# Forming the projected rows of six weight tiles inside the attention steps of a gated two-branch attention kernel

## The chip, the cores and the metric

One core of one Trainium2 chip runs the whole program. The metric is the time of one execution on the device in microseconds (us), the median of several runs. The engines named below are TensorE (PE, with its weight loads shown apart as PEld), VectorE (DVE), ScalarE (ACT), GpSimd (POOL) and SyncE (SP), which here only issues transfers. Each engine takes its instructions in the order in which the program was written.

## The reference

Two attention layers share one input `x` (2048 rows of 576). Layer A has 32 heads of 18, each with its own key and value. Layer B has 32 query heads that share one key and one value. The two outputs are mixed row by row with a gate.

```python
def _A_ref(x, wqkv, wo):
    qkv = transpose((x @ wqkv).reshape(B, S, 3, H, Dh), 2, 0, 3, 1, 4)
    scores = einsum("bhqd,bhkd->bhqk", q, k) * Dh ** -0.5
    o = einsum("bhqk,bhkd->bhqd", softmax(scores), v)
    return transpose(o, 0, 2, 1, 3).reshape(B, S, D) @ wo
...
def _B_ref(x, wq, wk, wv, wo):
    scores = einsum("bhqd,bkd->bhqk", q, k) * Dh ** -0.5     # k, v: one head for all
    o = einsum("bhqk,bkd->bhqd", softmax(scores), v)
...
g = sigmoid((x * gate_w).sum(-1, keepdims=True))
return g * A + (1 - g) * B
```

B = 1, S = 2048, D = 576, H = 32, Dh = 18, all in float32.

## The kernel before, in words

**Numbers in two halves.** TensorE multiplies a rounded form of float32. The kernel therefore splits every operand of a projection into a rounded high part and the low rest, and adds three products (high x high, low x high, high x low). `PROJ` (line 30) lists them: 14 matmuls make one block of a projection.

**Projection.** `wall` holds 14 weight tiles of 128 columns: the shared key, the gate, the shared value, then the 32 queries of layer B, then query and key of each head of layer A. Tile `mt` of the projection gives 128 rows of a DRAM table `qk_d`, each 2048 long, high and low part. `project` (line 144) forms one block of 512 columns of such a tile: 14 matmuls, then `leave` (line 159) copies the high part on ACT, subtracts on DVE for the low part and sends both to `qk_d` from POOL's queue (512 KB in one transfer). Tiles that hold keys also store a difference of two key blocks in `kd_d`.

The program has three parts before the attention steps reach their even pace:

1. Tiles 0 to 2, four blocks each, with `x` loaded and split as they go (lines 257 to 306).
2. "Phase one": tiles 3 to 9, 28 blocks one after the other (loop at line 347, `LEAD_T = MT - 4`). After each block `bring_row` issues one load, or two after the last block of a tile, that brings finished rows from `qk_d` back into SBUF: the shared key `ksb`, its difference `kdb` and the queries `qs` of the first three heads, 27 loads in all. The weights `wv` of layer A's values are also loaded, split on ACT and DVE and stored in a DRAM table `wv_d` (`load_wv`, `store_wv`).
3. "The lead": tiles 10 to 13, 16 blocks, each followed by six row-maximum blocks of the first heads (loop at line 814). `leave_lead` does the low parts on POOL. `store_x` writes the split `x` to the DRAM table `x_d`.

**Attention steps.** There are 64 heads (u = 0 to 31 for layer B, 32 to 63 for layer A) and 16 blocks of keys each, so 1024 steps, numbered T = 16u + block. A step forms four score blocks of 128 x 512 on TensorE (`step_scores`, line 526), takes four exponentials on ACT (line 538), multiplies them with the values (`step_pv`, line 541), and forms row maxima 22 steps ahead (`step_max`, line 466: matmul, then a reduce on DVE; every second step one block goes over ACT instead, line 481). When a head's maxima are complete, at steps T with T mod 16 = 10, `max_rows` (line 489) reduces and transposes them on DVE, splits them on POOL (`mh`, lines 497 and 118), writes them to DRAM and reads them back into two rows of `qs` on SP. The first scores of that head use these rows six steps later, at T mod 16 = 0.

**Order.** The schedule is written out by hand. Three strings give the order of the operations (lines 842 to 845): `PLAIN` covers two steps; `SPARSE` covers eight steps and carries one unit `U` of other work; `DENSE` covers two steps and carries one unit. Lines 918 to 927 choose the string by the step. Units come from generators in the list `todo`, one after the other:

- `value_units` (line 417), 32 units of 14 matmuls of 288 columns: layer A's values, with weights from `wv_d` and `x` from `x_d`. Steps 10 to 265 (`VB = 10`).
- `out_proj` (line 661), first segment: 32 units of 12 matmuls of 288 columns, steps 522 to 777 (`SEG`, line 786). The second segment runs under `DENSE` from step 946 on.

`begin` (line 849) runs, every second step, what is due: the loads of the next head's rows (`load_q`, `load_k`: issued on SP at T mod 16 = 0, line 766), the loads of values, and one step of the generators in `slow`. Those are `normalise` (line 590: divides eight heads' outputs by their sums and splits them on POOL) and `prep_wo` (line 647: splits the output weights on POOL). SP issues nearly all transfers, and a transfer that has to wait holds up those behind it.

Of the kernel before, what the change touches and what calls it, by code (L numbers as in the profile page):

```python
# [8 lines left out]
F32 = mybir.dt.float32  # L9
F32R = mybir.dt.float32r  # L10
# [32 lines left out]
def gated_mix_kernel(ctx: ExitStack, tc: tile.TileContext, xT, wall, wv, wo, out):  # L43
# [3 lines left out]
    def dma(o, i, eng=None):  # L47
        o, i = (x.bitcast(F32) if x.dtype == F32R else x for x in (o, i))
        return (eng or nc.sync).dma_start(o, i)
# [19 lines left out]
    wv_d = dram.tile([2, 2, P, NKT * 288], F32, name="wv_d")  # L69
    on_d = [dram.tile([9 * P, S], F32, name=f"on{x}") for x in "hl"]  # L70


# [146 lines left out]
    def bring_row():  # L219
        if rows_back:  # L220
            rows_back.pop(0)()

    with tc.tile_pool(name="xs", bufs=1, side="right") as xsp:
# [67 lines left out]
        for c in range(4):  # L291
            for mt in range(3):
# [14 lines left out]
    vws = ExitStack()  # L307
    vwp = vws.enter_context(tc.tile_pool(name="vwp", bufs=1, side="right"))


    def load_wv(hf):
        t = vwp.tile([P, NKT, 288], F32, name="vwst")
        load5(t, wv[:, 288 * hf:288 * hf + 288])
        return t

    def store_wv(hf, st):
        w = {y: vwp.tile([P, NKT, 288], F32R, name=f"vw{y}") for y in "hl"}
        split_w(st, w, nc.vector)
        for i, y in enumerate("hl"):
            dma(wv_d[hf, i], w[y].rearrange("p k f -> p (k f)"), nc.gpsimd)  # L320

    def store_x(i):
        y, c = "hl"[i % 2], i // 2
# [7 lines left out]
    for u in range(3):  # L331
        load_q(u, put=later)

    LEAD_T = MT - 4

    def tiles_left(WN):
        for mt in range(3, MT):
            w = WN
            if mt + 1 < MT:
                WN = prep_w(W.pop(0))  # L340
            if mt + 3 < MT:
                W.append(load_w(mt + 3))
            for c in range(4):
                yield mt, c, w

    left = tiles_left(WN)
    for n in range(4 * (LEAD_T - 3)):
        mt, c, w = next(left)
        if n in (0, 10):
            vs = load_wv(n // 10)  # L350
        project(mt, c, w)
        bring_row()
        if c == 3:
            bring_row()
        if n in (8, 18):
            store_wv(n // 10, vs)
    assert not rows_back
    vws.close()


    small = ctx.enter_context(tc.tile_pool(name="small", bufs=1, side="left"))
# [35 lines left out]
    def open_ph2():  # L397
        ph1.close()
        L["pt"].append(ctx.enter_context(tc.tile_pool(name="ppool", bufs=10, side="left")))
        L["work"] = ctx.enter_context(tc.tile_pool(name="work", bufs=2, side="left"))  # L400
        p2 = ctx.enter_context(tc.tile_pool(name="p2", bufs=1, side="right"))
        L["pool"] = p2
        L["ks"] = [p2.tile([P, S], F32R, name=f"ksa{i}") for i in range(2)] + [ksb]
        L["kds"] = [p2.tile([P, 512], F32R, name="kda"), kdb]

        L["early"] = ExitStack()
        L["vx"] = L["early"].enter_context(tc.tile_pool(name="vx", bufs=1, side="right"))
        for t in L["ks"][:2]:
            for b in (SB, MB):
                dma(t[b + 54:b + 56, :], ones_r)  # L410

    def open_oacc():
        L["early"].close()
        L["oacc"] = ctx.enter_context(tc.tile_pool(name="oacc", bufs=1, side="right")) \
            .tile([P, 16, D], F32, name="oacc")

    def value_units():

        pool = L["vx"]
        XV = {}  # L420

        def load(st_):
            XV[st_] = pool.tile([P, 2 * NKT - 1, P], F32R, name="xv", bufs=2)
            dma(XV[st_], x_d[:, :, st_ * P:(st_ + 1) * P])

        load(0)
        w = [{y: pool.tile([P, NKT, 288], F32R, name=f"vw{y}{hf}") for y in "hl"} for hf in range(2)]
        for hf in range(2):
            for i, y in enumerate("hl"):
                dma(w[hf][y], wv_d[hf, i].rearrange("p (k f) -> p k f", k=NKT))  # L430
        vst = [pool.tile([P, 16, 19], F32, name=f"vst{i}") for i in range(2)]
        for t in vst:
            nc.gpsimd.memset(t, 1.0)
        yield
        for st_ in range(16):
            if st_ < 15:
                load(st_ + 1)
            x = XV.pop(st_)
            for hf in range(2):
                fp = ps_m.tile([P, 512], F32, name="pm")  # L440
                for n, (a, b, k, kr) in enumerate(PROJ):
                    nc.tensor.matmul(fp[:, 0:288], x[:kr, k if b == "h" else NKT + k, :], w[hf][a][:kr, k, :],  # L442
                                     start=(n == 0), stop=(n == len(PROJ) - 1))
                nc.scalar.activation(vst[hf][:, :, 0:18], fp[:, 0:288].rearrange("p (h d) -> p h d", d=18), AF.Copy)
                dma(v_d[st_, :, 304 * hf:304 * hf + 304], vst[hf].rearrange("p h d -> p (h d)"))
                yield
# [214 lines left out]
    def out_proj(t0, rows, first=False):  # L661

        nt = len(rows)
        oacc = L["oacc"]
# [12 lines left out]

        load(0)
        yield
        w = WO[t0]  # L680
        for q in range(8):
            if q < 7:
                load(q + 1)
            o = {y: O[q, y] for y in "hl"}
            for s2 in range(2):
                st_ = 2 * q + s2
                for hf in range(2):
                    ops = [(o[b][:r, t, s2 * P:(s2 + 1) * P], w[a][:r, t, 288 * hf:288 * hf + 288])
                           for a, b in PRODS for t, r in enumerate(rows)]
                    fp = unit_bank()  # L690
                    for n, (x, y) in enumerate(ops):
                        nc.tensor.matmul(fp[:, 0:288], x, y, start=(n == 0), stop=(n == len(ops) - 1))  # L692
                    dst = oacc[:, st_, 288 * hf:288 * hf + 288]
                    if first:
                        nc.scalar.activation(dst, fp[:, 0:288], AF.Copy)
                    elif fin and hf == 0 and st_ in ON_ACT:
                        tmp = L["work"].tile([P, 288], F32, name="tmp", tag="ol", bufs=1)
                        nc.scalar.activation(tmp, fp[:, 0:288], AF.Copy)
                        nc.gpsimd.tensor_tensor(dst, tmp, dst, op=OP.add)
                    else:  # L700
                        nc.vector.tensor_tensor(dst, fp[:, 0:288], dst, op=OP.add)  # L701
                    if fin and st_ == 15:
                        dma(out[st_ * P:(st_ + 1) * P, 288 * hf:288 * hf + 288], dst, nc.sync if hf else nc.scalar)
                    elif fin and hf:
                        dma(out[st_ * P:(st_ + 1) * P, :], oacc[:, st_, :], nc.scalar if st_ in (8, 10, 12) else nc.sync)
                    yield
# [56 lines left out]
    def when(T, f):  # L763
        at.setdefault(T, []).append(f)
# [207 lines left out]
```

## Time and profile before

| what | value |
|---|---|
| median of 3 runs | 2738.71 us (2738.68 to 2739.05) |
| the profiled execution, its own time | 2739.16 us |
| span of the profiled execution, first to last instruction | 2737.4 us |
| granted TensorE clock | 1.000 |
| PE / PEld busy | 2729.2 / 1301.5 us |
| ACT / DVE / POOL busy | 2443.6 / 2391.7 / 271.4 us |
| moved by transfers | 242.09 MB, mean 88 GB/s |

The page gives each engine's busy time, a picture of the span in 40 slices, the chain of work that ended last, and groups of instructions by line. A busy PE is one that has matmuls in flight, not one at its peak. The timeline lists instructions by their start in the span, equal neighbours merged (start, length, engine, line, what is written from what, count). A waits view adds up who waited for whom. A windows view adds up each engine's busy time in a stretch, with the granted clock, the mean busy share of the 16 transfer engines and the bytes that they moved per second. Letters after an engine's name ("SPq", "POOLq") mark its queue of issuing instructions.

### The profile page before, as it was taken

What the parts mean: (1) busy time and instruction counts of PE and PEld (TensorE: products, weight loads), DVE (VectorE), ACT (ScalarE), POOL (GpSimd) and SP (SyncE); (2) the same over time, 40 slices, a digit from 0 to 9 for tenths busy, and PEclk for the clock granted to TensorE, in tenths of its full rate; (3) what the DMA queues carried; (4) which work ended last, traced back from release to release, by engine and by line L of the source; (5) the groups of instructions that cost most, each with busy time, mean ns of one, the idle gap of its engine ahead of it and who ended that gap; (6) DMA issues with size and microseconds to landing.
All of it is one profiled execution on the core that took longest, in us unless ns stands there. A gap on an engine that the chain in (4) does not pass through costs nothing.

```text
span 2737.4 us, 60422 instructions
## 1 busy us (share of the span) xinstructions
PE 2729.2 (100%) x23542; PEld 1301.5 (48%) x23542; DVE 2391.7 (87%) x4495; ACT 2443.6 (89%) x4787; POOL 271.4 (10%) x407
## 2 busy tenths in 40 slices
PE   9999999999999999999999999999999999999999
PEld 8874444454454333333334444444444333334555
DVE  4488888888889999999999898888989999998883
ACT  4338999999999999999999999999999999998776
POOL 2371000010001000100110001000100011011002
PEclk9999999999999999999999999999999999999999
DMA  8883211122111101211133213222321223224312
GB/s 285 326 303 125 60 55 38 59 80 75 42 57 57 56 27 34 65 48 31 47 95 108 87 58 95 93 70 75 100 87 46 68 86 99 67 79 120 101 46 89
DMA packets 145954, 242.09 MB, mean 88 GB/s; under 512 B 53650, under 2 KB 99810, under 8 KB 134092
## 3 DMA queue, kind: packets, MB, share of 16 engines
q1 hardware_dynamic: 131268, 187.13, 22.7%
q0 software_dynamic: 13504, 49.88, 4.8%
q8 instruction: 185, 3.03, 0.5%
q10 hardware_dynamic: 896, 1.23, 0.1%
q14 instruction: 101, 0.83, 0.1%
HBM read 149.61 MB, written 79.78 MB: 84 GB/s over the span
## 4 chain that ended last, share of the span: by engine, by line
PE 99%; DMA 0%; DVE 0%; ACT 0%; issue 0%; ACTq 0%
PE acc L544 38%; PE ps L530 32%; PE pm L478 14%; PE ps L156 6%; PE pm L692 4%; PE pm L442 2%; PE acc L555 1%; PE pm L530 0%; DMA xsh<-xT 0%; PE ps L478 0%; PE ps L692 0%; DVE mx L487 0%; DMA wst<-wall 0%; ACT pt L538 0%; DVE oacc L701 0%; PE pm L739 0%
## 5 line engine op out<-in xcount | busy, mean ns | idle before, releaser
L538 ACT ACTIVATE pt<-ps 128x512 f32<-128x512 f32 x4048 | 2133.8, 612 | 119.9 <-PE pm L478 55.3
L487 DVE TENSOR_REDUCE mx<-pm 128x1 f32<-128x512 f32 x3068 | 1942.5, 684 | 193.9 <-PE pm L478 145.7
L530 PE MATMUL ps<-qs,ksb 56*128 56x512 f32 x2688 | 899.2, 436 | 0.1
L478 PE MATMUL pm<-ksb,qs 54*128 54x512 f32 x2336 | 794.7, 437 | 0.1
L530 PEld LDWEIGHTS ps<-qs,ksb 56*128 56x128 f32 x2688 | 435.0, 184 | 493.8 <-ACT pt L538 465.0
L544 PE MATMUL acc<-pt,vb 128*19 128x256 f32 (+3 forms) x6656 | 579.3, 434 | 0.1
L544 PE MATMUL acc<-pt,vg 128*19 128x256 f32 (+3 forms) x6224 | 553.8, 443 | 0.0
L530 PE MATMUL ps<-qs,ksa 56*128 56x512 f32 x1360 | 454.6, 436 | 0.1
L478 PEld LDWEIGHTS pm<-ksb,qs 54*128 54x128 f32 x2336 | 370.9, 184 | 125.5 <-DVE mx L487 57.6
L478 PE MATMUL pm<-ksa,qs 54*128 54x512 f32 x1232 | 425.9, 439 | 0.0
L484 DVE CUSTOM_DVE_ANT_0 junk<-pm,xb 128x512 bf16<-128x512 f32 x500 | 340.3, 681 | 0.2
L530 PEld LDWEIGHTS ps<-qs,ksa 56*128 56x128 f32 x1360 | 219.4, 184 | 239.4 <-ACT pt L538 221.9
L481 ACT ACTIVATE xb<-pm 128x512 f32<-128x512 f32 x500 | 307.5, 615 | 0.0
L544 PEld LDWEIGHTS acc<-pt,vb 128*19 128x19 f32 x6656 | 125.6, 97 | 216.1 <-issue 192.7
L478 PEld LDWEIGHTS pm<-ksa,qs 54*128 54x128 f32 x1232 | 198.0, 184 | 56.5 <-DVE mx L487 26.0
L544 PEld LDWEIGHTS acc<-pt,vg 128*19 128x19 f32 x6224 | 118.8, 97 | 207.1 <-issue 183.2
L118 POOL CAST mh<-mt 128x32 fp32r<-128x32 f32 x64 | 13.4, 210 | 1719.7 <-DVE mt L495 1719.7
L478 PE MATMUL pm<-kdb,qs 54*128 54x512 f32 x372 | 153.3, 412 | 0.0
L162 ACT ACTIVATE phl<-ps 128x512 fp32r<-128x512 f32 x40 | 23.9, 598 | 71.4 <-PE ps L156 56.8
L156 PE MATMUL ps<-xh,wh 128*128 128x512 f32 (+1 forms) x300 | 85.6, 384 | 0.0
L156 PE MATMUL ps<-xh,wl 128*128 128x512 f32 (+1 forms) x300 | 83.3, 376 | 0.0
L168 DVE TENSOR_TENSOR phl<-ps,phl 128x512 fp32r<-128x512 f32 x40 | 27.7, 692 | 62.7 <-ACT phl L162 46.8
(144 smaller groups left out, 1471.9 us busy)
## 6 DMA issues: line engine op xcount, KB each, us to landing
qs<-qk SPq DMA_DIRECT2D x384, 144.0 KB
qk<-phl POOLq DMA_DIRECT2D x56, 512.0 KB, 5.6
ksa<-qk SPq DMA_DIRECT2D x132, 144.0 KB
ksb<-qk SPq DMA_DIRECT2D x66, 144.0 KB
xv<-x_d SPq DMA_DIRECT2D x16, 576.0 KB
onh<-oh SPq DMA_DIRECT2D x32, 256.0 KB
onl<-ol SPq DMA_DIRECT2D x32, 256.0 KB
oih<-onh SPq DMA_DIRECT2D x16, 512.0 KB
```

The source lines that it names most:

```text
L156: nc.tensor.matmul(fp[:, p0:p0 + g], w[a][:kr, k, :], X[b][:kr, k, x0 + p0:x0 + p0 + g], start=(n == 0), stop=(n == len(PROJ) - 1))
L168: nc.vector.tensor_tensor(hl[:, 1, :], fp, hl[:, 0, :].bitcast(F32), op=OP.subtract)
L442: nc.tensor.matmul(fp[:, 0:288], x[:kr, k if b == "h" else NKT + k, :], w[hf][a][:kr, k, :], start=(n == 0), stop=(n == len(PROJ) - 1))
L478: nc.tensor.matmul(pm, qs[u % 3][b:b + 54, i * P:(i + 1) * P], k, start=True, stop=True)
L481: nc.scalar.activation(MX["x", u, i], pm, AF.Relu)
L484: nc.vector.tensor_tensor_reduce(junk, pm, MX.pop(("x", u, i)), 1.0, -3e38, op0=OP.add, op1=OP.max, accum_out=MX[u][:, i, c:c + 1])
L487: nc.vector.tensor_reduce(MX[u][:, i, c:c + 1], pm, axis=AX.X, op=OP.max)
L530: nc.tensor.matmul(ps, kst(u)[b:b + 56, i * P:(i + 1) * P], qs[u % 3][b:b + 56, c * 512:(c + 1) * 512], start=True, stop=True)
L538: nc.scalar.activation(pt, ps, AF.Exp, scale=SCALE)
L544: nc.tensor.matmul(acc[32 * j:32 * j + 19, a:b], v_of(u, i), PT[u, i, j][:, a:b], start=(i == 0), stop=(i == 15), skip_group_check=True)
L555: nc.tensor.matmul(acc[32 * j:32 * j + 19, 256 * half + a:256 * half + b], v_of(NU - 1, i), pt[:, x + a:x + b], start=(i == 0), stop=(i == ...
L692: nc.tensor.matmul(fp[:, 0:288], x, y, start=(n == 0), stop=(n == len(ops) - 1))
```

## The change

Phase one ends after tile 3. `NT = 8` tiles are formed up front: tiles 0 to 2 as before, tile 3 alone in phase one (4 blocks), tiles 4 to 7 in the lead (16 blocks). The 27 loads that bring rows back are issued up to eight at a time after each of the four blocks of tile 3.

Tiles 8 to 13 become units of a new generator, `row_units`: seven units a tile, 42 in all, each 14 matmuls of 292 columns (296 in the seventh), steps 282 to 617 under `SPARSE`. A unit loads its columns of all nine split parts of `x` from `x_d` (128 partitions x 9 x 292 float32), ACT copies the result to SBUF, POOL splits it into high and low part, and SP stores it to `qk_d`. After the fourth unit of a tile POOL also forms and splits the key difference for `kd_d`. After the seventh POOL splits the next tile's weights.

The DRAM table `wv_d` goes. `value_units` loads `wv` itself at step 2 into the buffers named `vg`, and POOL splits it there. The value units move from steps 10 to 265 to steps 18 to 273. The first segment of the output projection moves from steps 522 to 777 to steps 634 to 889, and the split of the second segment's weights from step 862 to step 884.

```diff
-    for n in range(4 * (LEAD_T - 3)):
-        mt, c, w = next(left)
-        if n in (0, 10):
-            vs = load_wv(n // 10)
-        project(mt, c, w)
-        bring_row()
-        if c == 3:
+    for n in range(4 * (NT - 4 - 3)):
+        project(*next(left))
+        for _ in range(8):
             bring_row()
-        if n in (8, 18):
-            store_wv(n // 10, vs)
...
+    def row_units():
+
+        pool = L["px"]
+        XR, WR = [], []
...
+        def load_xr(c):
+            XR.append(pool.tile([P, 2 * NKT - 1, 296], F32R, name="xr", bufs=2))
+            n = 296 if c == 6 else 292
+            dma(XR[-1][:, :, 0:n], x_d[:, :, cut(c)])
...
+        def both(st, n):
+            hl = pool.tile([P, 2, 296], F32R, name="rhl", bufs=1)
+            split(st, hl[:, 0, 0:n], hl[:, 1, 0:n], nc.gpsimd, nc.gpsimd)
+            return hl[:, :, 0:n]
...
+        for mt in range(NT, MT):
+            rs = slice(mt * P, (mt + 1) * P)
+            first = pool.tile([P, 4, 292], F32, name="rst", bufs=1).rearrange("p c f -> p (c f)")
+            for c in range(7):
+                x = XR.pop(0)
+                if (mt, c) != (MT - 1, 6):
+                    load_xr((c + 1) % 7)
+                n = 296 if c == 6 else 292
+                fp = ps_m.tile([P, 512], F32, name="pm")
+                for i, (a, b, k, kr) in enumerate(PROJ):
+                    nc.tensor.matmul(fp[:, 0:n], w[a][:kr, k, :], x[:kr, k if b == "h" else NKT + k, 0:n],
+                                     start=(i == 0), stop=(i == len(PROJ) - 1))
+                b = (0, 292, 584, 876, 512, 0, 808)[c]
+                st = first[:, b:b + n]
+                nc.scalar.activation(st, fp[:, 0:n], AF.Copy)
+                dma(qk_d[:, rs, cut(c)].rearrange("a p f -> p a f"), both(st, n))
+                if c == 3:
+
+                    nc.gpsimd.tensor_tensor(first[:, 0:512], first[:, 512:1024], first[:, 0:512], op=OP.subtract)
+                    for i in range(2):
+                        d = both(first[:, 256 * i:256 * i + 256], 256)
+                        cs = slice(256 * i, 256 * i + 256)
+                        dma(kd_d[rs, 0:2, cs], d)
+                        dma(kd_d[rs, 2, cs], d[:, 0, :])
+                if c == 6 and mt + 1 < MT:
+                    w = next_w(mt + 1)
+                yield
...
-        for hf in range(2):
-            for i, y in enumerate("hl"):
-                dma(w[hf][y], wv_d[hf, i].rearrange("p (k f) -> p k f", k=NKT))
+
+        for hf in range(2):
+            src = wv[:, 288 * hf:288 * hf + 288]
+            main = src[0:512, :].rearrange("(p k) m -> p k m", p=P)
+            for k0, k1 in ((0, 3), (3, 5)):
+                t = L["pool"].tile([P, 16, 76], F32, name="vg", bufs=2)
...
+                split(t, w[hf]["h"][:, k0:k1], w[hf]["l"][:, k0:k1], nc.gpsimd, nc.gpsimd)
...
-    VB = 10
-    when(VB - 8, lambda: (todo.append(value_units()), pull(1)))
-    when(VB + 8 * 32 + 8, open_oacc)
-    SEG = ((0, [P] * 4, 450, 518), (4, [P] * 4, 862, 942))
+    VB = 18
+    when(2, lambda: (todo.append(value_units()), pull(1)))
+    RB = VB + 8 * 33
+    when(RB - 8, lambda: (early("px"), todo.append(row_units()), pull(1)))
+    RE = RB + 8 * 7 * (MT - NT)
+    when(RE, open_oacc)
+    SEG = ((0, [P] * 4, 450, RE + 12), (4, [P] * 4, 884, 942))
...
-        elif any(b <= T < b + 8 * 32 for b in (VB, SEG[0][3] + 4)):
+        elif VB <= T < VB + 8 * 32 or RB <= T < RE or SEG[0][3] + 4 <= T < SEG[0][3] + 4 + 8 * 32:
             emit(SPARSE, 1)
```

More of the change, by code (lines that the diff above doesn't have):

```diff
@@ L68, in gated_mix_kernel @@
     x_d = dram.tile([P, 2 * NKT - 1, S], F32, name="x_d")
-    wv_d = dram.tile([2, 2, P, NKT * 288], F32, name="wv_d")
     on_d = [dram.tile([9 * P, S], F32, name=f"on{x}") for x in "hl"]
@@ L306, in gated_mix_kernel @@
                         WN = prep_w(W.pop(0))
[L307 to L318, printed above, removed]
-        for i, y in enumerate("hl"):
-            dma(wv_d[hf, i], w[y].rearrange("p k f -> p (k f)"), nc.gpsimd)
     def store_x(i):
@@ L332, in gated_mix_kernel @@
         load_q(u, put=later)
-    LEAD_T = MT - 4
+    NT = 8
     def tiles_left(WN):
-        for mt in range(3, MT):
+        for mt in range(3, NT):
             w = WN
-            if mt + 1 < MT:
+            if mt + 1 < NT:
                 WN = prep_w(W.pop(0))
-            if mt + 3 < MT:
+            if mt + 3 < NT:
                 W.append(load_w(mt + 3))
@@ L410, in open_ph2, with early @@
                 dma(t[b + 54:b + 56, :], ones_r)
+    def early(name):
+        if "early" in L:
+            L["early"].close()
+        L["early"] = ExitStack()
+        L["px"] = L["early"].enter_context(tc.tile_pool(name=name, bufs=1, side="right"))
     def open_oacc():
@@ L415, in open_oacc, with cut, load_wr, next_w @@
             .tile([P, 16, D], F32, name="oacc")
+    def row_units():
+        pool = L["px"]
+        XR, WR = [], []
+        def cut(c):
+            return slice(292 * c, 292 * c + 292 if c < 6 else S)
+        def load_wr(mt):
+            WR.append(pool.tile([P, NKT, P], F32, name="wrst"))
+            load5(WR[-1], wall[mt])
+        def load_xr(c):
+            XR.append(pool.tile([P, 2 * NKT - 1, 296], F32R, name="xr", bufs=2))
+            n = 296 if c == 6 else 292
+            dma(XR[-1][:, :, 0:n], x_d[:, :, cut(c)])
+        def next_w(mt):
+            W = {y: pool.tile([P, NKT, P], F32R, name=f"wr{y}") for y in "hl"}
+            split(WR.pop(0), W["h"], W["l"], nc.gpsimd, nc.gpsimd)
+            if mt + 1 < MT:
+                load_wr(mt + 1)
+            return W
+        def both(st, n):
+            hl = pool.tile([P, 2, 296], F32R, name="rhl", bufs=1)
+            split(st, hl[:, 0, 0:n], hl[:, 1, 0:n], nc.gpsimd, nc.gpsimd)
+            return hl[:, :, 0:n]
+        load_wr(NT)
+        load_xr(0)
+        w = next_w(NT)
+        yield
[24 more added lines that the diff above has]
+                    w = next_w(mt + 1)
+                yield
@@ L417, in value_units @@
     def value_units():
-        pool = L["vx"]
+        pool = L["px"]
         XV = {}
@@ L679, in out_proj @@
         yield
-        w = WO[t0]
+        w, oacc = WO[t0], L["oacc"]
         for q in range(8):
```

11 lines of the change are left out of this document (6 added, 5 removed).

## The prediction

> **What bounds the kernel now.** I read the page first: engine totals, the slices, the chain that ended last.
>
> ```profile
> PE 2729.2 (100%) x23542; PEld 1301.5 (48%) x23542; DVE 2391.7 (87%) x4495; ACT 2443.6 (89%) x4787; POOL 271.4 (10%) x407
> ...
> PE   9999999999999999999999999999999999999999
> ...
> POOL 2371000010001000100110001000100011011002
> ...
> DMA  8883211122111101211133213222321223224312
> ...
> PE 99%; DMA 0%; DVE 0%; ACT 0%; issue 0%; ACTq 0%
> ```
>
> TensorE is on the path all along, POOL is nearly free, and the transfer engines are crowded only in the first three slices (some 200 us), where the change takes work away. A busy PE need not be at its peak, so the next view is of who waits, first in plain attention steps (steps 282 to 522), then in steps with value units.
>
> ```profile
> PEld ps L530 <- ACT pt L538: 239.0, 547, 0.8
> ```
> ```profile
> PEld ps L530 <- ACT pt L538: 83.7, 156, 0.8
> ```
>
> In 556 us of plain steps TensorE waits 239 us for score buffers that ACT has yet to empty; in 522 us with value units, 84 us. ACT's timeline in plain steps says why:
>
> ```profile
> 226.24 0.60 ACT L481 ACTIVATE xb<-pm 128x512 f32<-128x512 f32 x1
> 226.72 4.26 ACT L538 ACTIVATE pt<-ps 128x512 f32<-128x512 f32 x8
> 230.86 0.61 ACT L481 ACTIVATE xb<-pm 128x512 f32<-128x512 f32 x1
> ```
>
> Two steps take ACT 4.62 us without a gap. So ACT sets the plain pace, and a unit of matmuls put there first fills TensorE's waits. What a unit costs is read from POOL's `mh`, once per 16 steps (at T mod 16 = 10):
>
> ```profile
> 313.09 0.21 POOL L118 CAST mh<-mt 128x32 fp32r<-128x32 f32 x1 [39.71 <-DVE mt L495]
> ...
> 835.83 0.21 POOL L118 CAST mh<-mt 128x32 fp32r<-128x32 f32 x1 [39.83 <-DVE mt L495]
> ...
> 913.08 0.21 POOL L118 CAST mh<-mt 128x32 fp32r<-128x32 f32 x1 [27.15 <-DVE mt L495]
> ...
> 1469.21 0.21 POOL L118 CAST mh<-mt 128x32 fp32r<-128x32 f32 x1 [8.01 <-DVE mt L495]
> ...
> 1510.11 0.21 POOL L118 CAST mh<-mt 128x32 fp32r<-128x32 f32 x1 [40.35 <-DVE mt L495]
> ...
> 1549.79 0.21 POOL L118 CAST mh<-mt 128x32 fp32r<-128x32 f32 x1 [39.14 <-DVE mt L495]
> ...
> 2105.50 0.21 POOL L118 CAST mh<-mt 128x32 fp32r<-128x32 f32 x1 [39.11 <-DVE mt L495]
> ...
> 2142.66 0.21 POOL L118 CAST mh<-mt 128x32 fp32r<-128x32 f32 x1 [36.62 <-DVE mt L495]
> ```
>
> The first pair spans 13 blocks of 16 steps with value units (T = 42 to 250): 522.74 / 13 = 40.21 us. The second spans 15 plain blocks (T = 282 to 522): 37.08 us. Two units a block make 1.57 us per value unit. From 1549.79 to 2105.50 are 14 blocks with output units: 39.69 us, 1.31 per unit of 12 matmuls. The first block after plain steps (1469.21 to 1510.11) takes 40.90, 1.2 over the next; the first one back (to 2142.66) takes 37.16, 0.1 over plain.
>
> **The change part by part.** *Phase one loses 24 blocks.* ACT empties each block as TensorE ends it:
>
> ```profile
> 62.94 0.60 ACT L162 ACTIVATE phl<-ps 128x512 fp32r<-128x512 f32 x1 [2.57 <-PE ps L156]
> ...
> 129.13 0.60 ACT L162 ACTIVATE phl<-ps 128x512 fp32r<-128x512 f32 x1 [5.25 <-DMA qk<-phl]
> ...
> 139.15 0.60 ACT L162 ACTIVATE phl<-ps 128x512 fp32r<-128x512 f32 x1 [2.58 <-PE ps L156]
> ...
> 142.27 0.60 ACT L185 ACTIVATE pst<-ps 128x512 f32<-128x512 f32 x1 [1.90 <-PE ps L156]
> ```
>
> The fourth block ends at 62.94, the 28th at 139.15. The lead now follows the fourth: 139.15 - 62.94 = 76.2 us less (3.18 a block). ACT's 5.25 us wait for a store at 129.13 cost nothing, as 24 x 3.18 is the whole difference. The splits and stores of `wv` that go ran beside these matmuls: gain zero.
>
> *Steps 282 to 617 gain 42 units.* They come in the same string as the value units, with the same 14 matmuls. Widths are 292.6 columns in the mean against 288. TensorE's spacing gives the price of a column:
>
> ```profile
> 59.57 1.07 PE L156 MATMUL ps<-xh,wh 128*128 128x512 f32 x4
> 60.48 1.07 PE L156 MATMUL ps<-xh,wl 128*128 128x512 f32 x4
> ```
> ```profile
> 391.85 0.79 PE L442 MATMUL pm<-vwh,xv 128*128 128x288 f32 x4
> ...
> 393.89 0.49 PE L530 MATMUL ps<-qs,ksb 56*128 56x512 f32 x1
> ```
>
> Four matmuls of 512 columns start every 0.907 us, 0.44 ns a column at most; 14 x 4.6 columns add 0.03 us. So 1.57 + 0.03 = 1.60, and 42 x 1.60 = 67.0 us. Lower end: the output unit per matmul, 1.31 x 14 / 12 + 0.03 = 1.56, 65.3 us. Upper end: the whole 2.04 us that the value unit above held TensorE (391.85 to 393.89), 2.07 with the width, 86.9 us. I take the value unit, the same work in the same string. One more stretch of units means one more way in and out: 1.2 + 0.1 = 1.3 us. Moving the value and output units changes neither their number nor their price: 0.
>
> ACT gets one copy a unit, which fits: 4 x 4.62 + 0.41 = 18.9 us of ACT against 20.1 for eight steps.
>
> ```profile
> L120 POOL TENSOR_TENSOR ol<-ot,oh 128x512 fp32r<-128x512 f32 x32 | 41.1, 1285 | 3.7 <-DMA onl<-ol 1.3
> ...
> L118 POOL CAST oh<-ot 128x512 fp32r<-128x512 f32 x32 | 19.5, 610 | 203.5 <-DMA onh<-oh 202.9
> ...
> L444 ACT ACTIVATE vst<-pm 128x288 f32<-128x288 f32 x32 | 13.2, 412 | 15.6 <-PE pm L442 15.6
> ```
>
> *POOL and SP in these steps.* A split costs POOL (610 + 1285) / 512 = 3.7 ns a column: 1.1 us a unit, 3.2 more at a tile's fourth (difference 1.28, 512 columns split), 2.4 for the next weights; 79 us in 843. SP gets a load of 1.35 MB and a store a unit, and four stores at the fourth. What is queued behind them is the head's maximum row:
>
> ```profile
> 393.47 0.21 POOL L118 CAST mh<-mt 128x32 fp32r<-128x32 f32 x1 [39.65 <-DVE mt L495]
> ```
> ```profile
> 394.04 0.32 SPq L49 DMA_DIRECT2D m_d<-mh  x1
> 395.49 1.25 SPq L49 DMA_DIRECT2D qs<-m_d  x2
> 396.83 0.57 SPq L49 DMA_DIRECT2D xv<-x_d  x1
> ```
> ```profile
> qk<-phl POOLq DMA_DIRECT2D x56, 512.0 KB, 5.6
> ```
>
> POOL starts on that row at 393.47, and its way over DRAM ends some 1.1 us after 396.74 (the first half landed in 1.1: 394.36 to 395.49), so 4.4 us in all. It is needed six steps later, 6 x 2.51 = 15.1 us: 10.7 us spare. Every second unit is issued just behind the maximum row, the other one eight steps (20 us) ahead of the next. The worst is a fourth unit in that second place, as `rhl` is a single buffer: three splits (1.1 + 2 x 0.95), the difference, two landings of 5.6 between, behind a load of 1.35 MB at 324 GB/s (4.2): 4.3 + 11.2 + 4.2 = 19.7 us. It fits the 20, and 10.7 are spare: cost 0, with an upper end under the rivals. Row loads (`load_q`) come behind, at T mod 16 = 0, for use nine steps (22 us) later: 0.
>
> *Start of the values.* POOL's new splits of `wv` at step 2 are 2880 columns, 10.7 us, beside free POOL; with two waits for loads they end about 17 us after 217.7, at some 235.
>
> ```profile
> 217.68 0.60 SPq L49 DMA_DIRECT2D xv<-x_d  x1
> ```
> ```profile
> 231.46 0.21 POOL L118 CAST mh<-mt 128x32 fp32r<-128x32 f32 x1 [12.90 <-DVE mt L495]
> ```
>
> That makes the row of head 1 (231.46) some 3.5 us late, of 10.7 spare; the first value unit moves to step 18: 0.
>
> *Rows brought back.* They were spread over 28 blocks; now they stand in the first 14 us.
>
> ```profile
> 49.52 2.31 SPq L49 DMA_DIRECT2D ksb<-qk  x3
> ...
> 95.36 5.59 SPq L49 DMA_DIRECT2D qs<-qk  x5
> ```
> ```profile
> 63.00:139.00 76.00, 76.00 (x337) 62.99 (x336) 30.84 (x42) 26.23 (x42) 25.12 (x38) 1.00 0.86 324
> 139.00:218.00 79.00, 78.90 (x394) 54.25 (x396) 67.76 (x113) 31.64 (x58) 58.80 (x73) 1.00 0.78 291
> ```
>
> The lead's first maxima now come at 142.27 - 76.2 = 66 us and need 15 loads (ones, `ksb`, `kdb`, first `qs`). At 0.77 us each (three in 2.31) from 49 they are issued by 60.5, at 1.12 (five in 5.59) by 66; a landing follows. So they are in time, or late by one landing, 5.6. The transfer engines are 86% busy at 324 GB/s there; all 25 row loads of 147 KB are 3.7 MB, 11.4 us of that rate, less 14% of 14 us that were free: 9.4 us at most. I take 1.0, nearer the lower end, because the 5.25 us wait at 129.13, in the most crowded stretch, was made up in full.
>
> Sum against the profiled execution: 2739.2 - 76.2 + 67.0 + 1.3 + 1.0 = 2732.3 us. The median of the runs shown lies 0.45 below that execution, so 2731.8.
>
> **The rivals.** *A, columns conserved (no change).* 24 x 512 and 42 x 292.6 columns are both 12,288, times 14. If TensorE has no waits left to fill, a column costs the same 0.442 ns on both sides, 1.81 us a row unit and 76.1 us in all, 9.1 over the forecast: 2740.9. PE at 100% busy speaks for it; 1.57 per value unit, where 288 columns would give 1.78, against it. The Trainium skill, "TensorE: Matmul & The Clock Gate", section "Back-to-back issue gap", gives N / 2.4 + 2.5 ns for one matmul of N columns, which is the same rule: an estimate by it takes 72.5 us off and puts 73.1 on, 9.8 over the forecast, 2741.6. The trace differs, with 226 ns for 512 columns against its 216, and it shows the waits for ACT that the rule does not know.
>
> *B, the lead waits for its rows or its stores (no change).* The 9.4 us instead of 1.0: 2740.2. Crowded transfers speak for it, the made-up wait against it.
>
> *C, slower: the maximum row comes late.* POOL and SP take their work in order, so a row store that waits holds the row behind it. It decides from 10.7 us of lateness on: each microsecond above costs TensorE one, in up to 21 blocks. With load and store in front in every block (4.2 + 5.6) and one more landing of 1.1, lateness is 10.9 and costs 4 us; with a second load in front, 15.1, 4.4 x 21 = 92. The gain is lost from 11.0 on; at 11.4, which I take for this case, it costs 0.7 x 21 = 15 us: 2747. For it: `normalise` and the output weights also use POOL and SP at steps 357, 450, 469 and 581. Against it: in the value units SP has a load and a store in the same places, and `mh` keeps its distance.
>
> *D, slower: a row unit costs its full 2.07 us.* 19.9 more: 2751.7. From 1.76 us a unit on ((76.2 - 1.3 - 1.0) / 42) the change loses. Same evidence as A.
>
> **How the numbers follow.** The measurement tells from no change about 0.2%, 5.5 us: faster is below 2733.2, slower above 2744.2. Forecast 0.60, A 0.08, B 0.13, C 0.12, D 0.07. The forecast's own range is 2728 to 2735: units 1.7 less or 1.5 more, rows 0 to 3. Faster 0.60; A and B are the 0.21 of no change; C and D the 0.19 of slower. The range of 8 in 10 runs from 2727 to 2747: it takes in A, B and half of C, and leaves 0.05 below and 0.13 above.
>
> **What would show it.** Blocks of 16 steps between `mh` in steps 282 to 617 of 40.2 to 40.4 us (A: 40.7, D: 41.2; C: single blocks longer, with TensorE waiting for `qs`). The first copy of the lead at 66 us; B shows there, as gaps before the lead's matmuls or ACT waiting for `qk` stores. `mh` of head 1 some 3.5 us behind its transpose. POOL's busy time 60 to 90 us longer (79 + 10.7, less the stores that it no longer issues), and the plain blocks unchanged at 37.1. The prediction is wrong if the row units cost over 1.75 us each or the lead's start slips by more than 6 us.

## The result, and the profile after

| what | before | after |
|---|---|---|
| median | 2738.92 us (12 runs, 2738.62 to 2739.79) | 2744.90 us (12 runs, 2742.84 to 2747.54) |
| ratio, 95% interval | | 1.0023 [1.0015, 1.0030] |
| profiled execution | 2739.16 us, clock 1.000 | 2744.49 us, span 2742.7, clock 0.998 |
| POOL busy | 271.4 us | 342.6 us |
| moved by transfers | 242.09 MB | 293.74 MB |

The changed kernel is 6 us slower, 0.23%, where 6.9 us faster was forecast. The profiled execution is 12.2 us above the forecast sum of 2732.3. The page of the changed kernel, engine totals, slices and chain:

```profile
PE 2724.6 (99%) x24466; PEld 1359.9 (50%) x24466; DVE 2357.4 (86%) x4453; ACT 2442.2 (89%) x4787; POOL 342.6 (12%) x503
...
POOL 2810000100002111212121112000100010111002
...
DMA  8821111321124334444454444322322332224312
...
PE 97%; DMA 2%; DVE 1%; SPq 0%; issue 0%; ACT 0%; POOL 0%; POOLq 0%; DVEq 0%; ACTq 0%
```

TensorE still carries the chain, but 2% of it, where there was nothing, now runs through transfers: followed back, the chain leaves TensorE for loads and stores that it had to wait for. To place the loss, the steps are cut into blocks of 16 at the transpose of a head's maximum row on DVE. DVE's timeline of the changed kernel, at T = 298, 490, 506, 602 and 618 (start, length, engine, line, what is written from what):

```profile
879.86 0.21 DVE L549 STREAM_TRANSPOSE mt<-m 128x32 f32<-128x32 f32 x1
...
1363.02 0.21 DVE L549 STREAM_TRANSPOSE mt<-m 128x32 f32<-128x32 f32 x1
...
1408.31 0.21 DVE L549 STREAM_TRANSPOSE mt<-m 128x32 f32<-128x32 f32 x1
...
1649.99 0.21 DVE L549 STREAM_TRANSPOSE mt<-m 128x32 f32<-128x32 f32 x1
...
1696.14 0.21 DVE L549 STREAM_TRANSPOSE mt<-m 128x32 f32<-128x32 f32 x1
```

The first two stand 12 blocks apart: 483.16 / 12 = 40.26 us a block. From 1408.31 to 1649.99 are six blocks of 40.28. Between them stand two bad ones: 1363.02 to 1408.31 is 45.29 us, 1649.99 to 1696.14 is 46.15. They are 5.0 and 5.9 us over the others, so 10.9 of the 12.2 us lie in two blocks out of 21. One more is in the lead, where the first scores wait (a block of 42.2 against 41.2). ACT's and TensorE's timelines of the changed kernel have the lead's first copy and those scores:

```profile
65.94 0.60 ACT L184 ACTIVATE pst<-ps 128x512 f32<-128x512 f32 x1 [1.95 <-PE ps L155]
```
```profile
128.24 0.47 PE L584 MATMUL ps<-qs,ksb 56*128 56x512 f32 x1 [0.95 <-issue]
```

The copy stands where the forecast had it; the scores lose 0.95 us. All that TensorE's matmuls wait for transfers in steps 282 to 617, in the waits view (what waits, what it waits for: sum in us, times, longest):

```profile
PE pm L444 <- DMA xr<-x_d: 5.1, 3, 3.5
PE ps L584 <- DMA qs<-m_d: 1.5, 1, 1.5
```

`pm <- xr` is a row unit that waits for its columns of `x`; `ps <- qs` are a head's first scores, which wait for its maximum row. POOL's timeline of the changed kernel around the first bad block shows what held the maximum row (in brackets the idle time before an instruction and what ended it):

```profile
1335.26 0.40 POOL L117 CAST rhl<-rst 128x256 fp32r<-128x256 f32 x1 [8.62 <-DMA qk<-rhl]
...
1345.61 0.47 POOL L662 TENSOR_TENSOR sm<-sm,gt 112x128 f32<-112x128 f32 x1
1373.83 1.29 POOL L688 TENSOR_TENSOR ot<-ot,R 128x512 f32<-128x512 f32 x1 [27.75 <-DMA R<-r_d]
1375.05 0.23 POOL L117 CAST mh<-mt 128x32 fp32r<-128x32 f32 x1
```

POOL idles 27.75 us for the reciprocals `R` of `normalise`. The maximum row, transposed at 1363.23, stands behind that multiply and starts at 1375.05, 11.8 us late. In the kernel before, the same multiply, ahead of the row of T = 490, waited less, and that row (transposed at 1394.99) was 1.6 us late. POOL's timeline of the kernel before:

```profile
1395.38 1.29 POOL L634 TENSOR_TENSOR ot<-ot,R 128x512 f32<-128x512 f32 x1 [18.29 <-DMA R<-r_d]
1396.61 0.22 POOL L118 CAST mh<-mt 128x32 fp32r<-128x32 f32 x1
```

SP's timeline of the changed kernel shows why `R` and `x` come late:

```profile
1327.06 0.71 SPq L49 DMA_DIRECT2D qk<-rhl  x1
1336.50 4.72 SPq L49 DMA_DIRECT2D kd<-rhl  x4
1341.28 0.36 SPq L49 DMA_DIRECT2D kda<-kd  x1
1341.68 4.55 SPq L49 DMA_DIRECT2D qs<-qk  x6
1346.28 4.33 SPq L49 DMA_DIRECT2D ksa<-qk  x6
1350.71 2.96 SPq L49 DMA_DIRECT2D ot<-oe  x4
...
1354.80 1.53 SPq L49 DMA_DIRECT2D xr<-x_d  x1
1356.43 1.22 SPq L49 DMA_DIRECT2D qk<-rhl  x1
1357.75 0.60 SPq L49 DMA_DIRECT2D r_d<-sm  x1
1358.39 8.14 SPq L49 DMA_DIRECT2D R<-r_d  x8
```

This is a tile's fourth unit. Its store of `rhl` is issued at 1327.06, and the next store has to wait until that one has landed and POOL has refilled the single buffer (1335.26): SP issues nothing for 8.7 us. From 1336.50 to 1366.5 it then works off without a break what has gathered: the key differences, query rows, key rows, the outputs of a head, `x` for the next unit, and last the reciprocals. The load of `x` goes out at 1354.80, for a unit whose matmuls could start at 1361.75.

The wait for `R` is 9.5 us longer than before. From the instruction that forms the sums' quotient (ends 1346.08; before, 1377.09) to the issue of its store it takes 11.7 us instead of 4.3; this store and the eight loads take 8.8 us to issue instead of 6.8; the last landing takes 7.3 instead of 7.2. So 7.3 of the 9.5 us are time that the store stood in SP's queue. Why the loads issue more slowly isn't shown. Then TensorE's three waits, and the clock in the windows view (columns: length of the stretch in us, then busy time with the number of instructions of PE, PEld, DVE, ACT, POOL, then granted clock, DMA share, GB/s):

```profile
1363.08 0.77 PE L444 MATMUL pm<-xr,wrh 128*128 128x292 f32 x4 [1.33 <-DMA xr<-x_d]
...
1380.62 0.50 PE L584 MATMUL ps<-qs,ksb 56*128 56x512 f32 x1 [1.54 <-DMA qs<-m_d]
...
1652.22 1.31 PE L444 MATMUL pm<-xr,wrh 128*128 128x292 f32 x4 [3.51 <-DMA xr<-x_d]
```
```profile
1363.00:1380.50 17.50, 16.01 (x157) 8.09 (x157) 13.25 (x26) 13.90 (x28) 5.94 (x8) 1.00 0.25 63
1380.90:1384.30 3.40, 3.40 (x17) 1.32 (x16) 1.41 (x3) 1.73 (x4) 0.00 (x0) 0.50 0.74 236
1384.30:1408.00 23.70, 23.49 (x215) 11.73 (x212) 20.80 (x39) 21.64 (x43) 5.38 (x6) 1.00 0.78 245
...
1650.60:1657.40 6.80, 5.18 (x20) 4.25 (x20) 0.64 (x2) 1.09 (x3) 0.00 (x0) 0.50 0.64 175
```

The waits make 6.4 us, the blocks lost 10.9. Behind the wait of 1.54 us the granted clock is 0.50 for 3.4 us, and in and behind the one of 3.51 for 6.8, of which 5.2 are after the wait's end at 1652.2. Half of 3.4 and of 5.2 are 4.3 us: with the 6.4, 10.7. In the profile of before no stretch of half clock stands.

The theory from here: the units cost what was forecast, and SP's late loads cost time twice, once as a wait of TensorE and once as a clock halved behind it.

### The profile page after: what moved, and what is told of

Read it like the earlier page. It is cut to its first block, busy times and chain, and to the rows that moved or that the text cites. A ratio compares the mean times of both kernels' runs of the same rounds, so it can differ in the third digit from the quotient of the medians.

```text
span 2742.7 us, 62516 instructions
## 1 busy us (share of the span) xinstructions
PE 2724.6 (99%) x24466; PEld 1359.9 (50%) x24466; DVE 2357.4 (86%) x4453; ACT 2442.2 (89%) x4787; POOL 342.6 (12%) x503
## 2 busy tenths in 40 slices
DMA packets 205739, 293.74 MB, mean 107 GB/s; under 512 B 54738, under 2 KB 164642, under 8 KB 193868
## 4 chain that ended last, share of the span: by engine, by line
PE 97%; DMA 2%; DVE 1%; SPq 0%; issue 0%; ACT 0%; POOL 0%; POOLq 0%; DVEq 0%; ACTq 0%
PE acc L598 37%; PE ps L584 24%; PE pm L532 21%; PE pm L745 4%; PE ps L155 4%; PE pm L444 3%; PE pm L496 2%; DVE mx L541 1%; DMA xr<-x_d 1%; PE acc L609 1%; SPq L49 0%; PE pm L584 0%; DMA xsh<-xT 0%; DMA R<-r_d 0%; PE ps L532 0%; DMA r_d<-sm 0%
## 5 line engine op out<-in xcount | busy, mean ns | idle before, releaser
L532 PE MATMUL pm<-ksb,qs 54*128 54x512 f32 x2336 | 780.8, 433 | 0.4 <-DVE mx L541 0.2
L598 PE MATMUL acc<-pt,vb 128*19 128x256 f32 (+1 forms) x7120 | 568.9, 416 | 0.0
L532 PE MATMUL pm<-ksa,qs 54*128 54x512 f32 x1232 | 420.4, 436 | 0.0
L598 PEld LDWEIGHTS acc<-pt,vb 128*19 128x19 f32 x7120 | 144.6, 97 | 223.4 <-issue 188.0
L598 PEld LDWEIGHTS acc<-pt,vg 128*19 128x19 f32 x6432 | 127.2, 97 | 210.4 <-issue 181.1
L444 PE MATMUL pm<-xr,wrh 128*128 128x292 f32 (+1 forms) x378 | 70.0, 312 | 5.1 <-DMA xr<-x_d 5.1
L532 PEld LDWEIGHTS pm<-kdb,qs 54*128 54x128 f32 x372 | 68.4, 184 | 0.6
L117 POOL CAST rhl<-rst 128x292 fp32r<-128x292 f32 (+2 forms) x54 | 22.8, 421 | 346.6 <-ACT rst L448 275.0
L444 PEld LDWEIGHTS pm<-xr,wrh 128*128 128x128 f32 x378 | 55.4, 191 | 18.3 <-DVE mx L541 10.4
```

The lines of the kernel that those rows point to most:

```text
L117: eng_h.tensor_copy(h, src)
L444: nc.tensor.matmul(fp[:, 0:n], w[a][:kr, k, :], x[:kr, k if b == "h" else NKT + k, 0:n], start=(i == 0), stop=(i == len(PROJ) - 1))
L532: nc.tensor.matmul(pm, qs[u % 3][b:b + 54, i * P:(i + 1) * P], k, start=True, stop=True)
L598: nc.tensor.matmul(acc[32 * j:32 * j + 19, a:b], v_of(u, i), PT[u, i, j][:, a:b], start=(i == 0), stop=(i == 15), skip_group_check=True)
```

## The experiments

**e1, `x` loaded two units ahead.** The load for unit c + 2 goes out behind unit c's matmuls.

```diff
+        load_xr(1)
...
-                if (mt, c) != (MT - 1, 6):
-                    load_xr((c + 1) % 7)
...
+                if 7 * mt + c + 2 < 7 * MT:
+                    load_xr((c + 2) % 7)
```

> The changed kernel, in which a row unit now issues the load of x for the unit after the next one, behind its own matmuls, in place of the load for the next unit ahead of them. Theory 1 (the load of x stands too late in SP's order; the blocks of 16 steps at T = 490 to 506 and 602 to 618 lose their time to it and, at the first of them, to the late maximum row): TensorE's waits for xr, 5.1 us in three places, go to 0, and with them the half-clock stretch of 6.8 us (3.4 us of work lost); the wait of 1.5 us for the maximum row and its half-clock stretch stay, and at 602 to 618 a wait for the maximum row can come out from behind. So 5 to 9 us less than the changed kernel: 2736 to 2740. Theory 2 (the transfer engines are too full in these steps, whatever the order): the waits for xr stay within 2 us of what they were, time 2743 to 2747.

Measured: 2745.24 us (10 runs), 1.0020 [1.0011, 1.0029] against before: nothing gained. The waits for `x` are gone, as meant. In their place the maximum rows are later still, 13.85 and 12.9 us instead of 11.8 and 12.6, and now both cost. Timeline of TensorE:

```profile
1381.48 0.76 PE L585 MATMUL ps<-qs,ksb 56*128 56x512 f32 x1 [4.58 <-DMA qs<-m_d]
...
1669.51 0.47 PE L585 MATMUL ps<-qs,ksa 56*128 56x512 f32 x1 [3.23 <-DMA qs<-m_d]
```

The expectation of 2736 to 2740 was missed: both waits lie in the same blocks, and a TensorE that is held up by `x` comes later to the scores, so that the lateness of the maximum row had hardly shown.

**e2, the maximum row ahead of the multiply.** `normalise`'s first multiply is issued six steps later, so that POOL passes the maximum row first.

```diff
                 r0 += n
         yield
+        for _ in range(3 if 2 <= t <= 4 else 0):
+            yield
```

> The changed kernel, in which normalise of output tiles 2, 3 and 4 yields three times more between the loads of R and its first multiply on POOL, so that POOL's order has the next maximum row ahead of that multiply. Theory 1: the maximum row of T = 490 and 602 starts within 0.5 us of its transpose (11.8 us before at 490), TensorE's wait of 1.5 us for it and the half-clock stretch behind it go; the waits for xr (1.3 and 3.5 us) and the second half-clock stretch stay. 3 to 5 us less than the changed kernel: 2740 to 2742. Theory 2 (transfers too full): the row is early, but the waits for xr grow as the next thing that is late; time 2743 or more.

Measured: 2742.14 us (10 runs), 1.0009 [1.0000, 1.0019]; the profiled one 2742.80. No maximum row is waited for, and the waits for `x` stand, 3.40 and 3.58 us; the first of them was 1.33 in the changed kernel, and that it grew is what theory 2 had asked for. The median is 0.1 us above the range of theory 1, and the interval doesn't tell it from the kernel before. So each of the two repairs alone leaves the other cause in place.

**e3, both edits.**

> Both edits together. Theory 1: no wait of TensorE for a transfer in steps 282 to 617, all 21 blocks of 16 steps at 40.2 to 40.4 us, clock 1.000, and the time that the units' price alone gives: 2744.9 less 5.0 and 5.9 of the two long blocks, 2733 to 2735, 4 to 6 us faster than the kernel before. Theory 2 (transfers too full): at least one block stays over 42 us, time over 2739.

Measured: 2735.39 us (11 runs), 0.9987 [0.9978, 0.9996], 0.4 us above what was expected. The 21 blocks last 40.1 to 40.4 us, but for the block of entry with 41.4, and TensorE waits for no transfer in these steps. SP is still crowded: the row of T = 490 leaves POOL on time (1365.17), but its store stands behind the eight loads of `R`, and its rows are read back from 1375.88 on, 10.7 us after POOL's start where the prediction's rows had 2.0 (393.47 to 395.49). That is 8.7 us late, just inside the spare time (9.3 and 9.7 us by e1, worked out below). In these steps the two causes are the whole loss; the median is 9.5 us below the changed kernel's. It still misses the forecast by 3.6. In the profiled execution most of that lies at the start of the lead: head 0's maximum row is transposed at 117.34, 2.8 us later than in the changed kernel (114.50). TensorE's timeline and the windows of e3:

```profile
67.89 0.46 PE L533 MATMUL ps<-ksb,qs 54*128 54x512 f32 x1 [1.15 <-DMA qs<-qk]
```
```profile
60.00:69.40 9.40, 8.25 (x37) 6.14 (x36) 3.85 (x6) 3.05 (x5) 3.72 (x12) 1.00 0.76 308
69.50:72.90 3.40, 3.40 (x9) 2.64 (x9) 1.97 (x4) 0.00 (x0) 1.40 (x2) 0.50 0.88 353
73.00:80.00 7.00, 7.00 (x35) 4.79 (x34) 5.14 (x9) 2.46 (x4) 4.33 (x5) 1.00 0.90 331
```

The lead's first maxima wait 1.15 us for query rows brought back, and again 3.4 us of half clock follow (9 matmuls in them, against 35 in the next 7.0 us). The profiled executions of the changed kernel, e1 and e2 have the same program up to there and no such wait, so it differs from run to run.

**e4, the `wv` part alone,** on the kernel before: `wv_d` goes, `value_units` splits `wv` on POOL, and the value units move to step 18.

```diff
...
-    VB = 10
-    when(VB - 8, lambda: (todo.append(value_units()), pull(1)))
+    VB = 18
+    when(2, lambda: (todo.append(value_units()), pull(1)))
```

> The kernel before with one part of the change alone: wv is no longer split in phase one and stored, but loaded at step 2 into vg and split on POOL, and the value units start at step 18 in place of 10. The prediction put this at 0: the maximum row of head 1 comes 3 to 4 us late, of 10.7 to spare, and phase one keeps its pace, 2738.5 to 2739.5. Rival (part of the loss of the changed kernel starts here, as its block of steps up to T = 10 took 42.19 us against 41.2): 1 us or more slower, 2739.7 to 2741.

Measured: 2739.11 us (10 runs), 1.0000 [0.9991, 1.0009]. This part neither gains nor costs; the maximum row of head 1 is 4.7 us late, and TensorE does not wait for it.

**e5, the order of the rows brought back.** e3, and head 0's query rows are loaded right behind the shared key.

```diff
+    load_k(ksb, ROW_KB, put=later)
+    load_q(0, put=later)
     for b in (SB, MB):
         later(ksb[b + 54:b + 56, :], ones_r)
-    load_k(ksb, ROW_KB, put=later)
     load_kd(kdb, ROW_KB, put=later)
-    for u in range(3):
+    for u in range(1, 3):
```

> Both edits of the run before (x loaded two units ahead, normalise's first multiply behind the maximum row), and among the 27 loads that bring rows back the queries of head 0 now stand right behind the shared key; the rows of ones and kdb come behind them. Theory (rival B of the prediction at a small price: the lead's second maximum waits for the last rows of head 0, and a wait of 1.15 us there halved the clock for 3.4 us): the wait goes, the maximum row of T = 10 starts at 154.6 us in the span and not at 158.5, and runs spread less: 2731 to 2733 in all of them, against 2733 to 2738.5. Rival (the transfer engines are full there, and the order only moves the wait to a store or another load): T = 10 stays later than 156 us, or the time stays over 2734.

Measured: 2733.30 us (11 runs), 0.9979 [0.9970, 0.9988]. The wait at 67.89 and its half clock are gone, and the spread of the runs falls from 5.3 us (e3) to 1.4; as the wait wasn't in every execution, it is the spread that speaks for the edit. The result lies between the two sides: the median is 0.3 us above the 2731 to 2733 expected, and the row of T = 10 is transposed at 155.9 us, not 154.6. The block of the first scores is still 42.1 us long. TensorE idles 0.8 us ahead of them, until just after the last piece of the first maximum row has landed (127.28; the scores start at 127.37).

**e6, the row stores on POOL's queue,** one edit on the changed kernel, none of those above.

```diff
-                dma(qk_d[:, rs, cut(c)].rearrange("a p f -> p a f"), both(st, n))
+                dma(qk_d[:, rs, cut(c)].rearrange("a p f -> p a f"), both(st, n), nc.gpsimd)
...
-                        dma(kd_d[rs, 0:2, cs], d)
-                        dma(kd_d[rs, 2, cs], d[:, 0, :])
+                        dma(kd_d[rs, 0:2, cs], d, nc.gpsimd)
+                        dma(kd_d[rs, 2, cs], d[:, 0, :], nc.gpsimd)
```

> The changed kernel with one edit: the stores of the formed rows and key differences go out on POOL's queue, which forms them, and no longer on SP's. The loads of x stay where they were. Theory (SP is held at a row store until POOL's splits are done, up to 14 us at a tile's fourth unit, and what stands behind it, R, the head's rows and the load of x, comes late): R lands some 6 us earlier, the maximum rows of T = 490 and 602 are under 8 us late, waits for xr and for the row under 1 us together, time 2732 to 2737. Rival (R and x are late because there are too many bytes, 1.35 MB a unit): lateness over 10 us at T = 490 or 602 and a long block of over 43 us remain, time 2741 or more.

Measured: 2733.91 us (10 runs), 0.9980 [0.9971, 0.9989]: 11 us under the changed kernel. The same 293.74 MB move, in the same steps; the stores are issued by POOL and no longer by SP, and the transfers take 194,219 packets instead of 205,739. POOL's and SP's timelines of e6 at the first of the two places:

```profile
1368.16 1.29 POOL L688 TENSOR_TENSOR ot<-ot,R 128x512 f32<-128x512 f32 x1 [16.53 <-DMA R<-r_d]
1369.40 0.20 POOL L117 CAST mh<-mt 128x32 fp32r<-128x32 f32 x1
```
```profile
1328.58 10.68 SPq L49 DMA_DIRECT2D qs<-qk  x6
...
1348.33 2.16 SPq L49 DMA_DIRECT2D xr<-x_d  x1
...
1352.08 8.66 SPq L49 DMA_DIRECT2D R<-r_d  x8
```

SP starts on the query rows at 1328.58 instead of 1341.68; `x` goes out 6.5 us earlier, `R` 6.3 earlier, and POOL waits 16.5 us for it instead of 27.75. The maximum rows near the three `normalise` runs are 0.8 to 5.4 us late, which costs nothing, and the blocks are at 40.27 us. So it is the stores on SP's queue, and not the added 52 MB, that make the loads late. The edit takes two things off SP at once, the hold of 8.7 us and the issuing of the stores themselves (4.7 us for the four of `kd`); what each is worth alone isn't shown. POOL pays: issuing these 66 stores takes 46.7 us of its time, and it has that to spare.

**e7, maximum rows made late,** on the kernel before, to measure the spare time and the clock. POOL does idle subtractions ahead of `mh` in seven heads of plain steps, for a lateness of 9.8 to 19.2 us.

```diff
...
+    DLY = {19: 20, 21: 22, 23: 22, 25: 25, 27: 25, 29: 28, 31: 33}
...
+        if u in DLY:
+            nc.gpsimd.tensor_copy(dly[:, 0:32], mt)
+            for _ in range(DLY[u]):
+                nc.gpsimd.tensor_tensor(dly, dly, dly, op=OP.subtract)
```

> The kernel before, with nothing of the change: in seven heads among the plain steps POOL does 20, 22, 22, 25, 25, 28 and 33 idle subtractions of 0.46 us between the head's transpose and its maximum row (heads 19, 21, 23, 25, 27, 29, 31), so that the row comes 9.5, 10.4, 10.4, 11.8, 11.8, 13.1 and 15.4 us late. By the spare time of plain steps (6 x 2.31 less 4.4 = 9.5 us) TensorE waits about 0, 1, 1, 2.3, 2.3, 3.6 and 5.9 us, 16 us in all. Theory (a wait of TensorE of some 1.5 us or more halves its clock for one stretch of 3.4 us, which costs 1.7 us more): four or five half-clock stretches, 7 to 9 us, and 2762 to 2765 in all. Rival (only waits longer than 3.4 us halve the clock): one or two stretches, 2756 to 2759.

Measured: 2784.01 us in one run, beside 2739.22: more than either side expected. Waits, timeline of TensorE and windows of e7:

```profile
PE ps L538 <- DMA qs<-m_d: 31.7, 7, 10.9
```
```profile
965.39 0.76 PE L538 MATMUL ps<-qs,ksb 56*128 56x512 f32 x1 [1.96 <-DMA qs<-m_d]
...
1450.68 0.76 PE L538 MATMUL ps<-qs,ksb 56*128 56x512 f32 x1 [10.91 <-DMA qs<-m_d]
```
```profile
950.00:965.00 15.00, 13.44 (x120) 4.79 (x116) 13.14 (x26) 14.02 (x28) 8.60 (x23) 1.00 0.02 4
965.20:968.60 3.40, 3.21 (x14) 1.05 (x14) 1.90 (x4) 1.57 (x3) 0.00 (x0) 0.51 0.53 161
...
1443.10:1456.70 13.60, 6.02 (x30) 2.07 (x30) 3.64 (x7) 3.15 (x6) 5.83 (x11) 0.50 0.24 76
```

A row 9.77 us late costs a wait of 1.96, so the spare time in plain steps is 7.8 us (7.8 to 8.3 by the seven waits); the expectations had taken 9.5, and the last row ran into a `normalise` and came 19.2 us late. That is the first part of the miss. The second is the clock: all seven waits, of 1.96 to 10.9 us, come with a stretch of half clock of 3.4 us or a multiple (3.4, 3.4, 3.4, 6.8, 3.4, 6.8, 13.7). The waits add up to 31.7 us and the kernel is 44.8 longer. That leaves 13.1 us. Of the 40.9 us of half clock 11.7 lie in the waits themselves; half of the other 29.2 is 14.6, near the 13.1.

**e8, all repairs together:** the edits of e5 and e6.

> All four edits together: x loaded two units ahead, normalise's first multiply behind the maximum row, head 0's queries first among the rows brought back, row stores on POOL's queue. Theory (each edit alone or in pairs already took the waits of steps 282 to 617 away, so they do not add): within 1 us of the run with the first three, 2732 to 2734, clock 1.000 up to the last stretch. Rival (SP's stores also slow other work, which the waits hid): 2731.5 or less.

Measured: 2731.70 us (9 runs), before 2738.77, ratio 0.9974 [0.9964, 0.9984]. It beats both kernels, by 7.1 and 13.2 us; from e5 and e6 the intervals don't tell it apart. It is 1.6 us below e5, where up to 1 was expected, and 0.2 above the rival's 2731.5, so neither side is settled. No wait for a transfer is left in the steps; the lead keeps one gap of 1.1 us ahead of a score.

## Why the prediction was wrong

*Phase one, -76.2: right.* The lead's first copy came at 65.94 us (66 forecast), and near the lead's end head 0's maximum row is transposed 75.5 us earlier (114.50 for 189.98), rows brought back included.

*Row units at 1.60 us: right.* Twelve clean blocks of 40.26 us give (40.26 - 37.08) / 2 = 1.59 a unit, 66.8 for the 42. With that the rivals A (1.81, by columns conserved) and D (2.07) fall. So does the Trainium skill's price in "TensorE: Matmul & The Clock Gate", section "Back-to-back issue gap": by it the units give back all that phase one saves, and e8 keeps 7.1 us. The units do fill waits for ACT, as argued.

*Entry and exit, 1.3: right.* The block of entry is 1.15 us over its neighbours.

*Rows brought back, 1.0: about right.* The first maxima were as forecast; the first scores lost 1.0. In the profiled execution of e3 rival B shows at a small price, one late landing with a wait of 1.15 us and its half clock, not near 9.4.

*Start of the values, 0: right.* Maximum row 3.2 us late (3.5 forecast), and e4 measures no change.

*POOL and SP in these steps, 0: the step that failed.* It cost 10.9 us. POOL's time was right (+71 us of the 60 to 90). What was argued was one place as the worst for the maximum row, a fourth unit eight steps ahead of it: 19.7 us of work in a stretch of 20. In that place nothing was lost. A fourth unit stands there ahead of the rows of T = 314, 426 and 538, and all three start on time. POOL's timeline of the changed kernel at T = 314 (transpose from 920.09 to 920.30):

```profile
920.37 0.21 POOL L117 CAST mh<-mt 128x32 fp32r<-128x32 f32 x1 [2.11 <-DVE mt L549]
```

The two bad blocks come from a unit of the other kind, issued just behind a maximum row, which the prediction passed over: the fourth units at T = 474 and 586 hold SP, and the row that comes late is the next one, 16 steps on, at T = 490 and 602. The sum held the row's own queue, but not what else stands on SP in that stretch: six loads of query rows, six of key rows, and `normalise`'s. A third fourth unit, at T = 362, meets a `normalise` too, but no key rows, as layer B's heads share one key; the row of T = 378 is 5.9 us late there and nothing waits for it. The prediction called `load_q` free because its use is 22 us later, which is true of that load and not of those behind it. It also named `normalise` at 469 and 581 as evidence for C, without working out that POOL waits for `R` inside it, with the maximum row behind. And nothing in it had the unit's own load of `x` late behind SP.

*Rival C* was the right side with another mechanism, and that its 2747 lies near the measured 2744.9 is luck. It asked for lateness of more than 10.7 us in many blocks; 11.8 and 12.6 came in two, through `normalise`, with `x` late as well. The spare time of 10.7 was about a microsecond too long: the rows behind the waits in the changed kernel and e1 give 10.3, 9.3 and 9.7 us (11.8 - 1.54, 13.85 - 4.58, 12.9 - 3.23), the first of them with TensorE itself held up 1.33 us by `x`. Its price was too low, for the rule "each microsecond above costs TensorE one" leaves out the clock. The 6.4 us of waits cost 10.9.

What stays open: why the changed kernel's runs spread over 4.7 us and those of before over 1.2. Waits whose half-clock stretch is one or two units long would do that, and e5, which has no wait in the steps, spreads over 1.4; only one execution of each kernel has a trace, so it is argued, not shown.

## What to carry to other kernels

When work is moved into a steady stage, list everything on the in-order queue that issues its transfers, over the longest stretch in which one of them can wait, and ask of each item behind it when it is needed. A store that waits for a computation belongs on a queue with no urgent loads behind it: moving three lines of stores to another queue was worth 11 us here. And where several waits share a block, taking away one may only show the next (e1, e2), so they are tried together.

## What was not expected of the hardware

A short wait of TensorE can halve its clock. After waits of 1.15 us (e3), 1.54 us (changed kernel) and 1.96 us (e7) the granted clock was 0.50 for 3.4 us; one of 1.33 us (changed kernel, at 1363.08) left it at 1.00. The stretches in the steps are always 3.4 us or multiples (6.8, 13.7). The Trainium skill, "TensorE: Matmul & The Clock Gate", section "Part 1: The HAM clock gate (the "warmup" mystery)", has the clock halve after at least one idle window of about 3.4 us. The length of the stretches agrees with that window; these three waits are shorter than one window, the shortest a third of it.

How a wait lies in time counts too. Between the first stretch of full clock and the last matmuls, the clock changes only on a grid of 3.413 us in each trace: in e7 the half-clock stretches begin at 965.25 us and then 23, 23, 23, 24, 23 and 24 grid steps after one another. Each halving follows a grid window in which TensorE was idle for 1.15 us or more. The wait of 3.58 us in e2 shows it, cut at the grid in the windows view (columns as above):

```profile
1645.71:1649.12 3.41, 2.05 (x16) 0.74 (x14) 3.27 (x7) 3.11 (x7) 0.00 (x0) 1.00 1.00 303
1649.13:1652.54 3.41, 1.20 (x9) 1.23 (x10) 0.12 (x1) 0.26 (x1) 0.46 (x2) 1.00 0.69 183
1652.54:1655.95 3.41, 3.41 (x17) 2.20 (x20) 1.05 (x2) 1.50 (x4) 1.19 (x2) 0.50 0.62 146
1655.95:1659.36 3.41, 3.41 (x32) 1.15 (x28) 2.31 (x6) 2.95 (x7) 1.00 (x2) 1.00 0.18 46
```

The first window holds 1.37 us of the wait and the clock stays; the second holds 2.21 and the third runs at half clock. In these runs every full-clock window with 1.54 us of idle or more was followed by half clock and none with 1.11 or less; between them 1.15 was, 1.33 and 1.37 were not. What decides there no run here tells.
